# A gated attention and token-MLP block: cutting its last output tile at 384 of 512 columns, and loading W2 in eight DMAs instead of four

## The chip, the cores and the metric

The kernel runs on one core of one Trainium2 chip. The metric is the device time of one execution in microseconds (us).

Engine names in the profile: PE is TensorE (PEld its weight loads), DVE is VectorE, ACT is ScalarE, POOL is GpSimd, SP is SyncE, the engine that issues most of the DMAs here. A `q` after a name (SPq) marks what that engine's sequencer does.

## The reference

```python
# x: [1, 2048, 512] bf16. A: linear attention, 32 heads of 16. B: MLP over tokens, F = 1792.
g = sigmoid((x * gate_w).sum(-1, keepdims=True))
a = attention(x) @ wo                                  # [2048, 512]
u = gelu(einsum("bsd,sf->bdf", layernorm(x), w1) + b1)
b = (einsum("bdf,fs->bds", u, w2) + b2).transpose      # [2048, 512]
return g * a + (1 - g) * b
```

## The kernel before

The output is made in 16 tiles of 128 tokens and 512 columns. For each tile TensorE makes the attention part (`aps`, 4 matmuls) and the MLP part (`yps`, 14 matmuls over F = 14 x 128). ScalarE scales `aps` into `a_sc`, VectorE mixes `yps` and `a_sc` into `ot`, and SyncE stores `ot` by a DMA. The last tile is cut into two parts of 256 columns, so that only half a tile's mix and store follow the last matmul.

```python
NT, D, NF, P, SC, NSC, TPC = 16, 512, 14, 128, 512, 4, 4   # (from the shapes)
...
w2c = []

def load_w2(c):                              # chunk c of W2: 512 tokens, 1.75 MB
    w = wpool.tile([P, NT, FB * P], BF16, name="w2c", tag="wc")
    w2c.append(w)
    nc.sync.dma_start(out=w[:, :NF, :], in_=w2_view[:, :, c * SC : (c + 1) * SC])
...
for t in range(NT):
    c, tl = divmod(t, TPC)
    aps = bank("aps")
    for j in range(ND):
        mm(aps[:], pqT[:, j, t * P : (t + 1) * P], W2sb[:, j, :], j == 0, j == ND - 1)
    a_sc = work.tile([P, D], FP32, name="a_sc", tag="a_sc", bufs=2)
    nc.scalar.activation(out=a_sc[:], in_=aps[:], func=ACT.Identity,
                         scale=gg[:, t : t + 1], bias=c2[:, t : t + 1])
    parts = 2 if t == NT - 1 else 1
    W = D // parts
    for h in range(parts):
        cs = slice(h * W, (h + 1) * W)
        yps = bank("yps")
        for f in range(NF):
            mm(yps[:, :W], w2c[c][:, f, tl * P : (tl + 1) * P], uT[:, f, cs],
               f == 0, f == NF - 1)
        ot = opool.tile([P, D], BF16, name="ot", tag="ot")
        nc.vector.scalar_tensor_tensor(out=ot[:, :W], in0=yps[:, :W],
            scalar=c1[:, t : t + 1], in1=a_sc[:, cs], op0=ALU.mult, op1=ALU.add)
        nc.sync.dma_start(out=o_view[:, t, cs], in_=ot[:, :W])
    ...
```

What the source does not show: the framework gives each DMA that SyncE or ScalarE issues one of eight semaphores, in turn. (A semaphore is a counter that the landing of the DMA raises and that a waiting instruction tests.) At the end of the program SyncE waits for everything by a fixed list of nine waiting instructions. The second to the ninth hold the first to the eighth of these semaphores, always in that order (each also holds one other semaphore, met before). The built program shows that the last store of this kernel has the fourth semaphore, so it stands fifth in the list. Right after the list comes SyncE's first drain, the instruction that the times below call "the drain".

## Time and profile before

The median was 166.06 us in three runs (165.96 to 166.17). The profiled execution had a span of 164.0 us from its first to its last instruction.

These lines are from the page of the profile: the span, TensorE's busy time, the granted clock in 40 slices (tenths), the chain of work that ended last, the group of the mixes (busy us, mean ns of one, idle time before them and what ended it), and the DMA issues of W2 (count, KB each, median us from issue to landing).

```profile
span 164.0 us, 2057 instructions
PE 158.9 (97%) x771; PEld 74.1 (45%) x785; DVE 87.8 (54%) x200; ACT 58.7 (36%) x90; POOL 18.3 (11%) x37
PEclk9999999999999999999999999999999999999999
PE 95%; DMA 2%; issue 1%; ACT 0%; DVE 0%
L472 DVE SCALAR_TENSOR_TENSOR ot<-yps,c,a_sc 128x512 bf16<-128x512 f32 (+1 forms) x17 | 12.2, 719 | 46.1 <-PE yps L108 46.1
w2c<-in_B_w_dram SPq DMA_DIRECT2D x4, 1792.0 KB, 8.8
```

TensorE is busy 97% of the time and is nearly the whole chain. VectorE's 46.1 us of idle time before the mixes are waits for TensorE and cost nothing, except after the last matmul, when there is no more TensorE work to hide behind. So the timeline of the end is the view to read (start us, duration us, engine, line, operation, count, and in brackets the idle time before it):

```profile
157.54 3.22 PE L108 MATMUL yps<-uT,w2c 128*128 128x256 bf16 x28
157.71 3.93 SPq L476 DMA_DIRECT2D out_dram<-ot  x3
159.32 0.48 DVE L472 SCALAR_TENSOR_TENSOR ot<-yps,c,a_sc 128x256 bf16<-128x256 f32 x1 [1.64 <-PE yps L108]
160.80 0.48 DVE L472 SCALAR_TENSOR_TENSOR ot<-yps,c,a_sc 128x256 bf16<-128x256 f32 x1 [0.99 <-PE yps L108]
```

The last mix starts at 160.80 and takes 0.48 us. After it come the last store and the closing waits, over 2.5 us in which no compute engine works. How they stand can be seen when the view of SyncE's instructions at the closing line is asked for the stretch from the store's landing (162.84) to SyncE's drain (163.16). Its columns are the count, the duration in ns (least, median, most), and the first and last start in us:

```profile
L504 SPq EVENT_SEMAPHORE  x5: 28/28/28, 162.9 to 163.1; - x5
```

Five waiting instructions run after the landing. The first is the one that waited for it; the other four wait for nothing any more and still cost about 61 ns each, from one start to the next.

### The profile page before, as it was taken

To read this page: it belongs to the slowest core of one execution; us is meant where nothing else is said; L and a number is where in the kernel's file an instruction comes from. 1 tells how busy PE (TensorE), PEld (TensorE's weight loads), DVE (VectorE), ACT (ScalarE), POOL (GpSimd) and SP (SyncE) were. 2 spreads that over 40 slices of the span, in tenths; PEclk is the share of its full clock that TensorE was granted. 3 is DMA by queue.
4 is the path that set the end of the run, shared out by engine and by line. 5 is a ranking of instruction groups with operands and counts; after the bars stand their busy time and mean duration, and the time that the engine had idled before them with its cause. 6 is when DMAs were issued, how large, how long until landed. Compare 5 with 4: busy or idle time off the path is not lost.

```text
span 164.0 us, 2057 instructions
## 1 busy us (share of the span) xinstructions
PE 158.9 (97%) x771; PEld 74.1 (45%) x785; DVE 87.8 (54%) x200; ACT 58.7 (36%) x90; POOL 18.3 (11%) x37
## 2 busy tenths in 40 slices
PE   7999999999999999999999999999999999999992
PEld 2544444444544444434444444444444444444471
DVE  0599999958999999009994401256211111111131
ACT  3463386658577373212322113111122221111110
POOL 5000710200200000001055500050000000000000
PEclk9999999999999999999999999999999999999999
DMA  4999999999930005800993599932010011101001
GB/s 147 242 213 252 288 297 356 350 348 349 317 86 0 0 0 184 268 0 0 288 293 91 182 306 297 326 129 79 32 36 32 32 36 50 42 32 36 32 32 32
DMA packets 29993, 25.05 MB, mean 153 GB/s; under 512 B 7776, under 2 KB 29408, under 8 KB 29984
## 3 DMA queue, kind: packets, MB, share of 16 engines
q1 hardware_dynamic: 27968, 22.02, 45.0%
q0 software_dynamic: 1440, 2.38, 5.3%
q10 hardware_dynamic: 576, 0.52, 1.1%
q8 instruction: 6, 0.10, 0.3%
q14 instruction: 3, 0.02, 0.0%
HBM read 21.11 MB, written 2.23 MB: 142 GB/s over the span
## 4 chain that ended last, share of the span: by engine, by line
PE 95%; DMA 2%; issue 1%; ACT 0%; DVE 0%
PE uacc L108 29%; PE yps L108 29%; PE qacc L108 8%; PE gacc L108 8%; PE aps L108 8%; PE kacc L108 8%; DMA xs<-in_A_x_dram 2%; PE pt L194 1%; PE denps L108 1%; PE kvps L108 1%; PE wps L108 1%; ACT xT L198 0%; DVE ot L472 0%; PE zps L108 0%; PE pt L323 0%
## 5 line engine op out<-in xcount | busy, mean ns | idle before, releaser
L108 PE MATMUL uacc<-hs,w1c 128*128 128x512 bf16 x218 | 51.6, 379 | 0.4
L108 PE MATMUL yps<-uT,w2c 128*128 128x512 bf16 (+1 forms) x235 | 50.8, 366 | 0.2
L472 DVE SCALAR_TENSOR_TENSOR ot<-yps,c,a_sc 128x512 bf16<-128x512 f32 (+1 forms) x17 | 12.2, 719 | 46.1 <-PE yps L108 46.1
L108 PEld LDWEIGHTS <-w2c 128*128 128x128 bf16 x238 | 23.3, 98 | 25.3
L108 PEld LDWEIGHTS <-w1c 128*128 128x128 bf16 x224 | 21.6, 98 | 26.1 <-issue 0.4
L457 ACT ACTIVATE a_sc<-aps,c,gg 128x512 f32<-128x512 f32 x16 | 12.4, 778 | 46.7 <-PE aps L108 43.0
L317 ACT ACTIVATE uT<-uacc,bcol 128x512 bf16<-128x512 f32 x14 | 9.3, 687 | 27.7 <-PE uacc L108 27.7
L108 PE MATMUL qacc<-xT,wq_sb 128*128 128x512 bf16 x64 | 16.4, 379 | 0.0
L108 PE MATMUL aps<-W2sb,pqT 128*128 128x512 bf16 x62 | 16.2, 379 | 0.1
L108 PE MATMUL kacc<-wk_sb,xT 128*128 128x512 bf16 x63 | 15.9, 379 | 0.1
L108 PE MATMUL gacc<-pk,xs 128*128 128x512 bf16 x62 | 15.5, 379 | 0.1
L244 ACT ACTIVATE hs<-xs,nmr,rstd 128x512 bf16<-128x512 bf16 x16 | 12.8, 804 | 1.9 <-DVE nmr L238 1.9
L204 ACT ACTIVATE e<-qacc 128x512 bf16<-128x512 f32 x16 | 9.6, 597 | 10.1 <-PE qacc L108 10.1
L413 POOL DMA_DIRECT2D rex<-rd_dram x16 | 9.5, 603 | 23.0 <-DVE pqT L415 18.1
L204 ACT ACTIVATE e<-kacc 128x512 bf16<-128x512 f32 x16 | 9.3, 595 | 6.9 <-PE kacc L108 5.6
L208 DVE SCALAR_TENSOR_TENSOR pk<-kacc,e 128x512 bf16<-128x512 f32 x16 | 11.1, 692 | 0.6
L208 DVE SCALAR_TENSOR_TENSOR pqT<-qacc,e 128x512 bf16<-128x512 f32 x16 | 11.1, 692 | 0.6
L228 DVE BATCH_NORM_STATS2 stats<-xs 128x6 f32<-128x512 bf16 x16 | 10.9, 682 | 0.0
L205 DVE TENSOR_SCALAR e<-e 128x512 bf16<-128x512 bf16 x32 | 9.0, 281 | 3.1 <-ACT e L204 3.1
L400 DVE CUSTOM_DVE_ANT_0 junk<-xs,gw_b 128x512 bf16<-128x512 bf16 x16 | 9.8, 683 | 0.0
L108 PEld LDWEIGHTS <-xs 128*128 128x128 bf16 x64 | 6.3, 98 | 7.5
L108 PEld LDWEIGHTS <-pqT 128*128 128x128 bf16 x64 | 6.3, 98 | 7.6
(64 smaller groups left out, 73.2 us busy)
## 6 DMA issues: line engine op xcount, KB each, us to landing
w2c<-in_B_w_dram SPq DMA_DIRECT2D x4, 1792.0 KB, 8.8
w1c<-in_B_w_dram SPq DMA_DIRECT2D x2, 2048.0 KB, 15.5
w1c<-in_B_w_dram SPq DMA_DIRECT2D x3, 1024.0 KB, 12.3
rex<-rd_dram POOLq DMA_DIRECT2D x16, 128.0 KB, 2.9
out_dram<-ot SPq DMA_DIRECT2D x15, 128.0 KB, 1.7
xs<-in_A_x_dram SPq DMA_DIRECT2D x3, 512.0 KB, 5.3
wq_sb<-in_A_wqkv_dram SPq DMA_DIRECT2D x1, 512.0 KB, 6.9
wv_sb<-in_A_wqkv_dram SPq DMA_DIRECT2D x1, 512.0 KB, 10.9
```

The lines of the kernel that those rows point to most:

```text
L108: nc.tensor.matmul(o, lhsT=lhsT, rhs=rhs, start=start, stop=stop, **kw)
L194: nc.tensor.transpose(pt[:, k * P : (k + 1) * P], xs[:, t, k * P : (k + 1) * P], ident[:])
L204: nc.scalar.activation(out=e[:], in_=acc[:], func=ACT.Exp)
L205: nc.vector.tensor_scalar(out=e[:], in0=e[:], scalar1=1.0, scalar2=PHI_EPS, op0=ALU.min, op1=ALU.add)
L208: nc.vector.scalar_tensor_tensor(out=dst, in0=acc[:], scalar=0.0, in1=e[:], op0=ALU.max, op1=ALU.add)
L228: nc.vector.bn_stats(out=stats[:], in_=xs[:, t, :])
L244: nc.scalar.activation(out=hs[:, t, :], in_=xs[:, t, :], func=ACT.Identity, scale=rstd[:, t : t + 1], bias=nmr[:, t : t + 1],)
L317: nc.scalar.activation(out=uT[:, j, :], in_=acc[:], func=ACT.Gelu_apprx_tanh, bias=bcol[:, j : j + 1])
L400: nc.vector.tensor_tensor_reduce(out=junk[:], in0=xs[:, t, :], in1=gw_b[:], scale=1.0, scalar=0.0, op0=ALU.mult, op1=ALU.add, accum_out=gp ...
L413: nc.gpsimd.dma_start(out=rex[:], in_=src.unsqueeze(1).to_broadcast([8, HEAD, SC]))
L457: nc.scalar.activation(out=a_sc[:], in_=aps[:], func=ACT.Identity, scale=gg[:, t : t + 1], bias=c2[:, t : t + 1],)
L472: nc.vector.scalar_tensor_tensor(out=ot[:, :W], in0=yps[:, :W], scalar=c1[:, t : t + 1], in1=a_sc[:, cs], op0=ALU.mult, op1=ALU.add,)
```

## The change

Two edits, both aimed at what follows the last matmul. The last tile is cut into 384 and 128 columns, so that the last mix and the last store are smaller. And each W2 chunk comes in two DMAs: not for the sake of the loads, but because four more DMAs turn the eight semaphores by half a round, which puts the last store on the eighth, whose wait is the last of the list.

```diff
     def load_w2(c):
         w = wpool.tile([P, NT, FB * P], BF16, name="w2c", tag="wc")
         w2c.append(w)
-        nc.sync.dma_start(out=w[:, :NF, :], in_=w2_view[:, :, c * SC : (c + 1) * SC])
+        for f0 in (0, NF // 2):
+            f1 = f0 + NF // 2
+            nc.sync.dma_start(
+                out=w[:, f0:f1, :], in_=w2_view[:, f0:f1, c * SC : (c + 1) * SC]
+            )
...
-        parts = 2 if t == NT - 1 else 1
-        W = D // parts
-        for h in range(parts):
-            cs = slice(h * W, (h + 1) * W)
+        for c0, W in ((0, D - P), (D - P, P)) if t == NT - 1 else ((0, D),):
+            cs = slice(c0, c0 + W)
             yps = bank("yps")
```

## The prediction

> **What bounds the kernel.** TensorE. The page gives PE 97% of a 164.0 us span at full granted clock; the chain that ended last is 95% PE. In the last stage 512-column matmuls start every 216 ns without a hole, so only what follows the last matmul, 3.4 us, can move much. In the trace: the last matmul starts at 160.49; the last VectorE mix (128x256, 0.484 us) at 160.80; its store is issued at 161.31 (0.333 us) and lands by 162.84, 1.53 us after the issue's start. SyncE then ends a list of nine closing waits about 61 ns apart. Four pass before the landing; the fifth holds the last store's semaphore and passes at 162.86; four more follow, to 163.10; the drain is at 163.16, the end at 163.99.
>
> **What the change does.**
>
> 1. *Closing waits.* The new program has four more loads on SyncE. DMA semaphores go round eight in turn, so the last store moves from the fourth to the eighth, which stands last in the closing list. The four waits after the landing become waits before it: eight at 61 ns from about 161.5 end near 162.0, in free time. Saving 163.10 - 162.86 = 0.24 us, on the critical path.
>
> 2. *Smaller last mix.* 0.752 us for 512 columns and 0.484 us for 256 give, by a line, 0.35 us for 128 and 0.62 us for 384 (estimate). Saving 0.13 us. The 384-column mix would end near 160.6, before the last starts at 160.8, and its store's issue near 161.0, before the last store's at 161.2: it blocks nothing.
>
> 3. *PE in the last tile.* Now 28 matmuls of 256 columns at 109 ns. The 128-column matmuls of the key-value product start every 55.5 ns: 14 x (162 + 55.5) against 28 x 109, no change within 0.03 us.
>
> 4. *Smaller last store.* One DMA engine's eight data packets take 188 ns at 512 B and 358 ns at 1 KB; eight of 256 B should take about 105 ns (estimate), 0.08 us less. But the Trainium skill ("DMA: Bandwidth & Descriptors", Specifications) says that below 512 B the engine does a read-modify-write. No 256 B store is in this trace; I let it take back half: 0.04 us saved.
>
> 5. *W2 in two pieces.* Same bytes, same 1 KB rows; four more issues of 0.37 us on an idle SyncE, four more waits on a weight load. Chunks are issued from 61.9 to 98.6 us, land 8 to 11 us later, are first read at 99, 114, 130 and 146 us. Such waits cost PE nothing now. Worth 0.
>
> **Sum.** 0.24 + 0.13 + 0.04 = about 0.41 us: span about 163.6, measured 166.06 to **165.65 us**, eight times in ten between 165.45 and 165.95. Chances: faster by over 2% 0.005, within 2% 0.985, slower 0.01.
>
> **What would show it.** The ninth closing wait is the one that ends with the landing, and the drain follows within 0.1 us (1). The last mix is 128x128, about 0.35 us, from near 160.8 after the 384-column one (2, 3). Landing 1.4 to 1.55 us after the last issue's start (4); over 1.6 us would be small rows or queueing. PE idle at the W2 matmuls stays near 0.2 us (5).
>
> **What would make it wrong.** A read-modify-write of 0.2 us or more; the two last stores, 0.5 us apart instead of 1.5, queueing; SyncE or VectorE still busy with the 384-column part; the run-to-run spread (0.2 us over three runs).

## The result, and the profile after

The changed kernel took 165.69 us in the median (165.30 to 166.15, six runs); before, with the three further runs of the same rounds, took 166.10 us (165.96 to 166.50, six runs). The ratio is 0.9976, with a 95% interval of 0.9956 to 0.9996. By the 2% mark that is "same"; the interval just excludes no gain at all.

From the page of the changed kernel:

```profile
span 163.6 us, 2078 instructions
PE 159.9 (98%) x785; PEld 73.6 (45%) x785; DVE 87.8 (54%) x200; ACT 58.7 (36%) x90; POOL 18.3 (11%) x37
PE 98%; DVE 0%; issue 0%
L474 DVE SCALAR_TENSOR_TENSOR ot<-yps,c,a_sc 128x512 bf16<-128x512 f32 (+2 forms) x17 | 12.2, 720 | 45.9 <-PE yps L108 45.8
w2c<-in_B_w_dram SPq DMA_DIRECT2D x8, 896.0 KB, 7.5
```

The span is 0.4 us shorter. (TensorE's larger busy time is no extra work: the trace of before lacks the records of 14 matmuls, 771 instead of 785.) The end of the timeline, where the 28 matmuls of the last tile carry the form of the first of them:

```profile
157.55 3.22 PE L108 MATMUL yps<-uT,w2c 128*128 128x384 bf16 x28
157.73 3.81 SPq L478 DMA_DIRECT2D out_dram<-ot  x3
160.09 1.08 DVE L474 SCALAR_TENSOR_TENSOR ot<-yps,c,a_sc 128x384 bf16<-128x384 f32 x2 [2.39 <-PE yps L108]
```

TensorE's stretch is as long as before (3.22 us). The two mixes now stand close together, from 160.09 to 161.16. Narrowed to the end, the same view shows the last of them alone:

```profile
160.73 0.81 SPq L478 DMA_DIRECT2D out_dram<-ot  x2
160.81 0.35 DVE L474 SCALAR_TENSOR_TENSOR ot<-yps,c,a_sc 128x128 bf16<-128x128 f32 x1
```

It starts when the last mix started before, and takes 0.35 us instead of 0.48 us. And SyncE at its closing line, from the landing of the last store (162.65) to the drain (162.75):

```profile
L506 SPq EVENT_SEMAPHORE  x1: 27/27/27, 162.7 to 162.7; - x1
L506 SPq DRAIN  x1: 7/7/7, 162.8 to 162.8; - x1
```

One waiting instruction after the landing instead of five. The trace's own records of the closing list say the same in starts, us. The first wait, which holds no semaphore of the eight, passed at 161.687 and 161.587.

| wait for semaphore | before | changed |
|---|---|---|
| 1st | 161.751 | 161.651 |
| 2nd | 161.813 | 161.713 |
| 3rd | 161.877 | 161.777 |
| 4th | **162.858** (last store) | 161.839 |
| 5th | 162.917 | 161.898 |
| 6th | 162.979 | 161.959 |
| 7th | 163.038 | 162.374 (384-column store) |
| 8th | 163.099 | **162.671** (last store) |
| drain | 163.164 | 162.751 |
| end | 163.994 | 163.610 |

To compare kernels without the noise of their beginnings, times are counted below from the first `yps` matmul of the last tile. That point lies 147.70 to 147.71 us after the first `gacc` matmul in all 13 profiled kernels; `gacc` itself starts between 9.60 and 10.17 us, depending on when the first loads land.

| from the trace, us | before | changed |
|---|---|---|
| last tile's first matmul to last matmul | 2.947 | 3.000 |
| last tile's first matmul to last mix | 3.258 | 3.258 |
| last mix | 0.484 | 0.352 |
| issue of the last store to its landing | 1.532 | 1.462 |
| landing to SyncE's drain | 0.323 | 0.097 |
| drain to end | 0.830 | 0.859 |
| **last tile's first matmul to end** | **6.456** | **6.056** |

The gain at the end is 0.400 us: 0.132 of the mix, 0.070 of the store, 0.226 of the waits, less 0.029 that reappears after the drain. These make 0.399; the remaining 1 ns is the step from the mix to the issue.

### The profile page after: what moved, and what is told of

It is laid out like the page before. It is cut to its first block, busy times and chain, and to the rows that moved or that the text cites. A ratio compares the mean times of both kernels' runs of the same rounds, so it can differ in the third digit from the quotient of the medians.

```text
span 163.6 us, 2078 instructions
## 1 busy us (share of the span) xinstructions
PE 159.9 (98%) x785; PEld 73.6 (45%) x785; DVE 87.8 (54%) x200; ACT 58.7 (36%) x90; POOL 18.3 (11%) x37
## 4 chain that ended last, share of the span: by engine, by line
PE 98%; DVE 0%; issue 0%
PE uacc L108 30%; PE yps L108 30%; PE kacc L108 9%; PE aps L108 8%; PE qacc L108 8%; PE gacc L108 8%; PE wps L108 2%; PE pt L194 1%; PE denps L108 1%; PE kvps L108 1%; DVE ot L474 0%; PE zps L108 0%; PE pt L323 0%
## 5 line engine op out<-in xcount | busy, mean ns | idle before, releaser
L108 PE MATMUL yps<-uT,w2c 128*128 128x512 bf16 (+2 forms) x238 | 51.0, 366 | 0.0
L474 DVE SCALAR_TENSOR_TENSOR ot<-yps,c,a_sc 128x512 bf16<-128x512 f32 (+2 forms) x17 | 12.2, 720 | 45.9 <-PE yps L108 45.8
L108 PEld LDWEIGHTS <-w2c 128*128 128x128 bf16 x238 | 22.8, 98 | 25.9
L269 DVE TENSOR_TENSOR zacc<-zacc,pk 128x512 f32<-128x512 f32 x14 | 9.6, 686 | 0.2
L108 PEld LDWEIGHTS <-wq_sb 128*128 128x128 bf16 x64 | 6.3, 98 | 7.5
```

Of the source, the lines that this page charges most:

```text
L108: nc.tensor.matmul(o, lhsT=lhsT, rhs=rhs, start=start, stop=stop, **kw)
L269: nc.vector.tensor_tensor(out=zacc[:], in0=first, in1=pk[:, t, :], op=ALU.add)
```

## The experiments

Main theory: the terms add, and the order of the closing waits is the largest of them. Rival A: the smaller last piece is all, and the waits would be hidden by something else. Rival B: the finer W2 loads feed TensorE sooner. The first four runs shared a chip and eleven runs of before; the next three and the last four likewise.

### The changed kernel again

No edit.

> The changed kernel once more, to have it timed beside the parts on one chip. All theories: ratio to before near 0.9976 (0.996 to 0.999). In the trace, from the start of the last mix to SyncE's drain: 1.94 us as in its first profile (2.37 us before), of which landing to drain 0.10 us (0.32 us before), mix 0.35 us (0.48 us before), issue to landing 1.46 us (1.53 us before), each within 0.05 us.

Measured: 165.81 us (165.25 to 166.12, six runs) against 166.28 us, ratio 0.9972 (0.9950 to 0.9993). Last mix to drain 1.943 us, landing to drain 0.097, mix 0.351, issue to landing 1.467. So the end repeats within 5 ns, although this execution's span was 0.3 us longer. Where that came from is a line of its timeline of TensorE near the start:

```profile
6.24 0.81 PE L108 MATMUL kacc<-wk_sb,xT 128*128 128x512 bf16 x3 [0.37 <-DMA wk_sb<-in_A_wqkv_dram]
```

TensorE waited 0.37 us for a first load of the attention weights, and the first `gacc` started at 10.13 instead of 9.85 us. Variations of this kind are as large as the whole effect, and no part of the change touches them.

### W2 in two pieces alone

```diff
 # last tile as before: 256 and 256 columns
-        nc.sync.dma_start(out=w[:, :NF, :], ...)
+        for f0 in (0, NF // 2): nc.sync.dma_start(out=w[:, f0 : f0 + NF // 2, :], ...)
```

> W2 in two pieces each, last tile still in 256 and 256 columns. Main theory (order of the closing waits): landing to drain falls from 0.32 to 0.08-0.10 us; mix stays 0.48 us and issue to landing 1.53 us; last mix to drain 2.13-2.15 us, so some 0.23 us less than before, ratio near 0.9986. Rival A (all the gain is the smaller last piece): landing to drain may change, but last mix to drain stays within 0.05 us of 2.37, ratio 1.000. Rival B (finer W2 loads feed TensorE sooner): the last matmul starts over 0.1 us earlier than in before.

Measured: 165.87 us (165.48 to 166.14), ratio 0.9978 (0.9957 to 0.9999). SyncE at its closing line from the landing (162.842) to the drain:

```profile
L508 SPq EVENT_SEMAPHORE  x1: 28/28/28, 162.9 to 162.9; - x1
L508 SPq DRAIN  x1: 13/13/13, 162.9 to 162.9; - x1
```

Landing to drain is 0.097 us; mix (0.485) and landing (1.533) are as before; last mix to drain is 2.143 us, 0.225 less than before, as the main theory said. Rival A falls. Rival B falls too: the last matmul starts at 160.484 us, in before at 160.485, with the first `gacc` at 9.833 in both. Time comes back after the drain here as well (0.866 us, 0.036 more than in before), so to the end the gain is 0.188 us (6.268 against 6.456).

### The 384 and 128 columns alone

```diff
 # W2 in one piece as before
-        parts = 2 if t == NT - 1 else 1
+        for c0, W in ((0, D - P), (D - P, P)) if t == NT - 1 else ((0, D),):
```

> 384 and 128 columns, W2 in one piece each; the last store has the fourth semaphore again. Main theory: mix 0.35 us, issue to landing 1.46 us, but landing to drain 0.32 us as before: last mix to drain about 2.17 us, so 0.20 us less than before, ratio near 0.9988. Rival A: the whole 0.4 us, ratio near 0.9976. There is one catch: the 384-column store now has the third semaphore and lands 0.3 us before the last one, so it should not matter.

Measured: 165.98 us (165.49 to 166.19), ratio 0.9981 (0.9961 to 1.0001). From the landing (162.730) to the drain:

```profile
L502 SPq EVENT_SEMAPHORE  x5: 28/28/28, 162.7 to 163.0; - x5
L502 SPq DRAIN  x1: 7/7/7, 163.1 to 163.1; - x1
```

Mix 0.351, issue to landing 1.483, landing to drain 0.323 us: last mix to drain 2.184, expected about 2.17. To the end it gains 0.184 us (6.272). The two halves of the change make 0.188 + 0.184 = 0.372 us of its 0.400 us. Most of the rest is the scatter of one landing: the same last store took 1.483 us here and 1.462 us in the changed kernel. The timed runs cannot tell either half from the whole.

### The same turn of the semaphores without touching W2

```diff
 # W2 whole, last tile 256 and 256 columns
-            nc.sync.dma_start(out=o_view[:, t, cs], in_=ot[:, :W])
+            if 8 <= t < 12:
+                nc.sync.dma_start(out=o_view[:, t, 0:P], in_=ot[:, 0:P])
+                nc.sync.dma_start(out=o_view[:, t, P:D], in_=ot[:, P:D])
+            else:
+                nc.sync.dma_start(out=o_view[:, t, cs], in_=ot[:, :W])
```

> W2 whole and 256 and 256 columns as before; instead tiles 8 to 11 are each stored by two DMAs (128 columns, then 384), which also makes four more DMAs and moves the last store to the eighth semaphore. Main theory: the same as e1 in the tail: landing to drain 0.08-0.10 us, last mix to drain 2.13-2.15 us, ratio near 0.9986. Rival B: nothing gained, 1.000. It also gives four stores of 256-byte rows with no store of the same time ahead: if these rows cost a read-modify-write, they land no sooner after their issue than 512-byte rows (1.53 us); if they go by size, about 1.45 us.

Measured: 165.69 us (165.38 to 166.46), ratio 0.9975 (0.9950 to 0.9999). Landing to drain 0.081 us, last mix to drain 2.126 us (expected 2.13 to 2.15), to the end 6.221 us: 0.235 us less than before, with W2 as it was. So it is the count of DMAs that matters, not what they carry. This time no 0.03 us came back after the drain (0.835).

The four stores of 256-byte rows in the middle of the stage landed 1.44 to 1.47 us after the start of their issue, the last 512-byte rows of this run 1.53 us, the 1 KB rows before and after them in this stage 1.69 to 1.71 us (apart from the first three stores of the stage, which took longer). The store's DMA line and the landing line of the view of the output tile, narrowed to the first of them:

```profile
L477 SPq DMA_DIRECT2D out_dram<-ot x1: 333/333/333, 134.7 to 134.7; - x1
DMA to landing us min/median/max: 1.5/1.5/1.5
```

The trace has 1.474 us for this one. Time goes by size down to 256 bytes a row; no read-modify-write penalty shows.

### One more load: the last store on the first semaphore

```diff
 # the changed kernel, W2 chunk 0 in three pieces
-        for f0 in (0, NF // 2):
+        for f0, f1 in ((0, 5), (5, 10), (10, NF)) if c == 0 else ((0, 7), (7, NF)):
```

> The changed kernel, but the first W2 chunk comes in three pieces: one more load, and the last store moves on from the eighth semaphore to the first, which stands second of the nine closing waits. Main theory: seven waits are left after the landing, so landing to drain is 7 x 0.061 + 0.08 = about 0.5 us (0.10 us in the changed kernel), last mix to drain about 2.35 us (1.94 us): the change's whole gain is given back, ratio to before near 1.000. Mix 0.35 us and issue to landing 1.46-1.48 us unchanged. Rival A (order of waits is worth nothing): last mix to drain stays at 1.94 us and the ratio near 0.9975. Rival B (finer W2 loads): the same or a little better than the changed kernel.

Measured: 166.81 us (166.40 to 167.06) against 166.23 us, ratio 1.0031 (1.0016 to 1.0046). This is slower than expected; the ratio near 1.000 was missed. From the landing (162.565) to just after the drain:

```profile
L505 SPq EVENT_SEMAPHORE  x8: 27/28/28, 162.6 to 163.0; - x8
L505 SPq DRAIN  x2: 13/72/130, 163.1 to 163.6; - x2
```

Eight waits stand after the landing (the one that it released, and seven more); landing to drain is 0.559 us, last mix to drain 2.392 us. That much was expected (0.5 and 2.35 us), and rivals A and B are refuted once more. But then SyncE stands: its first drain is at 163.12 and its second only at 163.59. In the other kernels there are 0.05 to 0.08 us between these two. Drain to end became 1.350 us instead of 0.859.

I then looked at SyncE's instructions in the traces of all kernels, counted from the first recorded one. Each kernel with 82 or 83 of them (changed, again, `e1`, `e4`, `e5`, `e6`) has a gap of 0.45 to 0.48 us before its 80th. In the changed kernel the 80th is the wait for a release that the other engines pass 0.33 us earlier (162.956 against 163.289), and all but about 0.03 us of the pause is hidden. In `e4`, one instruction longer, the 80th is the drain by which SyncE reports to the others, and nothing hides it. The kernels with 75 to 79 (before, `e2`, `e3`) do not reach that place. (Their last instruction also has 0.45 to 0.46 us before it, but that is a wait for GpSimd's last release, which ScalarE, VectorE and TensorE pass within 12 ns of SyncE.) This was a new theory: the pause belongs to a place in SyncE's program. `e7`, `e8` and `e9` below test it.

### A still smaller last piece: 448 and 64 columns

```diff
-        for c0, W in ((0, D - P), (D - P, P)) if t == NT - 1 else ((0, D),):
+        for c0, W in ((0, D - 64), (D - 64, 64)) if t == NT - 1 else ((0, D),):
```

> The changed kernel with 448 and 64 columns: where does a smaller last piece stop paying? By the line through the measured mixes the 448-column mix takes 0.69 us and the 64-column one 0.28 us; the rows of the last store are 128 B. If the mix were all (naive reading): 0.07 us less from last matmul to drain. I expect a loss: TensorE has at most 14 x 55 = 0.78 us of work after the 448 columns (less if 64-column matmuls go faster), the 448-column mix is not done before the last one could start, and SyncE still issues its store (0.33 us) then. The last mix starts 0.2 to 0.35 us later than in the changed kernel, counted from the first matmul of the last tile, the last store is issued over 0.2 us later in spite of the shorter mix. Issue to landing 1.40-1.46 us. The spacing of the 64-column matmuls (27 ns if by columns, 55 ns if the weights set a floor) is measured by the way.

Measured: 165.75 us, a single run. The end of its timeline:

```profile
157.43 3.22 PE L108 MATMUL yps<-uT,w2c 128*128 128x448 bf16 x28
160.33 0.88 DVE L474 SCALAR_TENSOR_TENSOR ot<-yps,c,a_sc 128x448 bf16<-128x448 f32 x2 [2.76 <-PE yps L108]
```

The last mix takes only 0.275 us, but it starts 3.506 us after the last tile's first matmul instead of 3.258, behind the 448-column mix (0.684 us). The last store is issued at 4.041 us instead of 3.638, behind the issue of the 448-column store. Issue to landing was 1.474 us, a little over the expected range. To the end it takes 6.477 us: the whole gain of the change is gone. The 64-column matmuls started every 29 to 30 ns, so new weights set no floor of 55 ns.

### Three parts: 256, 160 and 96 columns

```diff
-        for c0, W in ((0, D - P), (D - P, P)) if t == NT - 1 else ((0, D),):
+        for c0, W in ((0, 256), (256, 160), (416, 96)) if t == NT - 1 else ((0, D),):
 # and W2 chunk 3 in one piece, so that there are four extra DMAs again
```

> A try at beating both: the last tile in 256, 160 and 96 columns, three W2 chunks in two pieces, so that the last store stays on the eighth semaphore. If 96-column matmuls start every 41 ns, TensorE's work is unchanged; the 160-column mix (0.38 us) is done before the last starts; the last mix takes 0.32 us (0.35 us), the 192-byte rows land 0.01-0.02 us sooner: last tile's first matmul to drain 0.04 to 0.06 us shorter than in the changed kernel, far too little for the timed runs to tell (ratio near 0.997). If weights set a floor of 55 ns, the 96-column part takes 0.2 us longer on TensorE and the version loses 0.15 us against the changed kernel.

Measured: 165.75 us (165.37 to 166.06) against 166.23 us, ratio 0.9968 (0.9952 to 0.9984). From its timeline:

```profile
160.21 0.38 DVE L473 SCALAR_TENSOR_TENSOR ot<-yps,c,a_sc 128x160 bf16<-128x160 f32 x1 [0.43 <-PE yps L108]
160.80 0.32 DVE L473 SCALAR_TENSOR_TENSOR ot<-yps,c,a_sc 128x96 bf16<-128x96 f32 x1 [0.21 <-PE yps L108]
```

VectorE is idle for 0.21 us before the last mix, so the part ahead does not block it; the 96-column matmuls start every 42 to 43 ns. Last tile's first matmul to drain is 5.158 us, 0.039 us less than in the changed kernel (5.197), just under the 0.04 to 0.06 us expected; to the end 6.018 us.

### The extra DMAs as stores, with 384 and 128 columns

```diff
 # the changed kernel, with W2 whole again
-        for f0 in (0, NF // 2): ...
+        nc.sync.dma_start(out=w[:, :NF, :], in_=w2_view[:, :, c * SC : (c + 1) * SC])
 # and the stores of e3
+            if 8 <= t < 12:
+                nc.sync.dma_start(out=o_view[:, t, 0:P], in_=ot[:, 0:P])
+                nc.sync.dma_start(out=o_view[:, t, P:D], in_=ot[:, P:D])
```

> The changed kernel with its four extra DMAs made otherwise: W2 whole, tiles 8 to 11 stored by two DMAs each; 384 and 128 columns, last store on the eighth semaphore. SyncE's program is three instructions shorter than in the changed kernel. Theory of the place in the program (SyncE stands for 0.45-0.48 us before its 80th recorded instruction, in every kernel that has 82 or more of them): with 79 the pause is not there, drain to end 0.83 us (0.86 us), landing to drain 0.08 us, last tile's first matmul to end 6.00-6.02 us (6.06 us in the changed kernel). Rival (the pause belongs to the finer W2 loads or to the semaphore's place): 6.06 us again. Ratio near 0.997.

Measured: 165.85 us (165.61 to 166.13) against 166.17 us, ratio 0.9984 (0.9969 to 0.9999). SyncE has 79 recorded instructions and no pause; drain to end 0.836 us, landing to drain 0.081 us. Last tile's first matmul to end is 6.026 us, 6 ns outside the expected range and 0.030 us less than in the changed kernel. Of this gain 0.023 us lie after the drain; 0.016 us lie before it (0.081 against 0.097, for a reason that no run shows), and 0.009 us are lost again in the landing.

### Five extra loads, the fifth issued by ScalarE

```diff
 # e4, but:
+            q = nc.scalar if (c, f0) == (0, 10) else nc.sync
-            nc.sync.dma_start(
+            q.dma_start(
                 out=w[:, f0:f1, :], in_=w2_view[:, f0:f1, c * SC : (c + 1) * SC]
```

> The kernel with five extra loads (last store on the first semaphore), but the fifth of them issued by ScalarE, so that SyncE's program is as long as in the changed kernel. Separates two costs that came together there: seven waits left after the landing, and 0.45 us that SyncE stood between its two drains. Theory of the place in the program: landing to drain 0.50-0.56 us as there, but drain to end 0.86 us in place of 1.35 us; ratio to before near 1.000 in place of 1.003. Rival (the 0.45 us comes with the semaphore's place): drain to end 1.35 us, ratio 1.003.

Measured: 166.04 us (165.89 to 166.23, five runs) against 166.17 us, ratio 0.9996 (0.9981 to 1.0010). From the landing (162.405) to just after the second drain:

```profile
L506 SPq EVENT_SEMAPHORE  x8: 28/28/28, 162.4 to 162.9; - x8
L506 SPq DRAIN  x2: 7/7/7, 163.0 to 163.0; - x2
```

Eight waits and 0.559 us to the drain as in `e4`, but both drains within 0.06 us, and drain to end 0.866 us. The pause moved back behind the second drain, before SyncE's 80th instruction. The two costs that came together in `e4` are separated: the place of the semaphore gives back the whole gain of the change and 0.068 us more (6.524 us to the end, 6.456 in before), and the one instruction more in SyncE's program costs another 0.476 us (7.000).

### Twelve extra loads

```diff
-        for f0 in (0, NF // 2):
+        for f0, f1 in ((0, 4), (4, 8), (8, 11), (11, NF)):
```

> The changed kernel with each W2 chunk in four pieces: twelve extra loads instead of four, so the last store is on the eighth semaphore again, and SyncE's program is eight instructions longer than the changed kernel's. Theory of the place: the pause of 0.45 us is still before the 80th recorded instruction, which is now the fourth closing wait, before the landing: hidden; drain to end 0.83 us, last tile's first matmul to end 6.02-6.04 us. Rival (the pause is tied to the end of the program): 6.06 us, pause after the second drain. Main theory of the closing waits: landing to drain 0.08-0.10 us whether four or twelve loads are extra.

Measured: 165.72 us (165.43 to 165.82, five runs), ratio 0.9972 (0.9958 to 0.9987). SyncE has 90 recorded instructions. The gap of 0.44 us stands before the 80th, now the fourth closing wait (162.006 to 162.450), before the landing at 162.909, where it costs nothing. Landing to drain 0.082, drain to end 0.830 us; to the end 6.013 us, a little better than expected. The pause is tied to the place, not to the end of the program, and a full extra turn of the semaphores changes nothing.

### The best of both

```diff
 # e7, but:
-            if 8 <= t < 12:
+            if 8 <= t < 11:
-        for c0, W in ((0, D - P), (D - P, P)) if t == NT - 1 else ((0, D),):
+        for c0, W in ((0, 256), (256, 160), (416, 96)) if t == NT - 1 else ((0, D),):
```

> The best of both: last tile in 256, 160 and 96 columns, W2 whole, tiles 8 to 10 stored by two DMAs each (three extra DMAs and one of the last tile). Last tile's first matmul to end 5.96-5.98 us: 6.018 us of the three parts with W2 loads, less 0.03 us of the pause and 0.016 us of landing to drain. Before has 6.456 us, the changed kernel 6.056 us. Ratio near 0.9965; against the changed kernel the timed runs cannot tell 0.08 us.

Measured: 165.66 us (164.98 to 165.92) against 166.17 us, ratio 0.9965 (0.9946 to 0.9985). The landing of its last two stores, from the view of the output tile narrowed to them:

```profile
L478 SPq DMA_DIRECT2D out_dram<-ot x2: 332/332/332, 161.0 to 161.5; - x2
DMA to landing us min/median/max: 1.4/1.5/1.5
```

Last tile's first matmul to end is 5.979 us, within the range expected, 0.477 us less than before and 0.077 us less than the changed kernel. In the traces it is the shortest of all. The timed runs do not tell it from the changed kernel, so that it beats the changed kernel is shown for the end of the trace only. (With 80 recorded SyncE instructions its 80th is the last wait of all, where a pause and the wait for GpSimd cannot be told apart.)

The ends of all thirteen traces together, in us:

| kernel | waits after landing | mix | issue to landing | landing to drain | drain to end | last tile's first matmul to end |
|---|---|---|---|---|---|---|
| before | 5 | 0.484 | 1.532 | 0.323 | 0.830 | 6.456 |
| changed | 1 | 0.352 | 1.462 | 0.097 | 0.859 | 6.056 |
| `e0` changed again | 1 | 0.351 | 1.467 | 0.097 | 0.859 | 6.061 |
| `e1` W2 only | 1 | 0.485 | 1.533 | 0.097 | 0.866 | 6.268 |
| `e2` split only | 5 | 0.351 | 1.483 | 0.323 | 0.829 | 6.272 |
| `e3` more stores | 1 | 0.484 | 1.534 | 0.081 | 0.835 | 6.221 |
| `e4` first semaphore | 8 | 0.351 | 1.455 | 0.559 | 1.350 | 7.000 |
| `e5` 448 and 64 | 1 | 0.275 | 1.474 | 0.096 | 0.866 | 6.477 |
| `e6` three parts | 1 | 0.318 | 1.423 | 0.096 | 0.860 | 6.018 |
| `e7` stores, 384 and 128 | 1 | 0.351 | 1.471 | 0.081 | 0.836 | 6.026 |
| `e8` fifth on ScalarE | 8 | 0.351 | 1.462 | 0.559 | 0.866 | 6.524 |
| `e9` twelve loads | 1 | 0.350 | 1.462 | 0.082 | 0.830 | 6.013 |
| `e10` stores, three parts | 1 | 0.316 | 1.421 | 0.082 | 0.839 | 5.979 |

## Why the prediction was right or wrong

The predicted time was 165.65 us with a range of 165.45 to 165.95; measured were 165.69 us and, in the later rounds, 165.81 us. The mechanism was right, and the terms were nearly the right size.

1. **Closing waits: right.** 0.24 us was predicted; landing to drain fell by 0.226 us. The built program shows the order of the semaphores, and the trace of before shows the price of a wait, so this could be computed. `e1` and `e3` show the term alone, `e4` and `e8` reverse it. Two things were missed beside it. The list does not end near 162.0 us: the eighth wait stops for the 384-column store until 162.374, still 0.28 us before the landing. And 0.029 us come back after the drain, because the longer SyncE program runs into the pause that `e7` to `e9` place.
2. **Smaller last mix: right.** 0.13 us predicted by a line through two measured sizes, 0.132 measured (0.484 to 0.352). The 384-column mix and its store's issue block nothing, as said: the last mix starts 3.258 us after the tile's first matmul in both kernels. `e5` shows where that ends.
3. **TensorE in the last tile: right.** The spacing is 162 to 163 and 55 to 56 ns, as estimated. The last matmul starts 0.053 us later, but as a shorter one it is done at the same time.
4. **Smaller last store: right in sign, too small.** 0.04 us predicted, 0.070 measured (0.049 to 0.077 over the seven traces with this last store). The half that I gave to the read-modify-write, which the Trainium skill states ("DMA: Bandwidth & Descriptors", Specifications), did not appear: 1.462 us for 256-byte rows against 1.532 for 512-byte rows, and 1.44 to 1.47 with no store just ahead (`e3`). The DMA records agree: from the first data packet to the first semaphore packet, which is the time of one DMA engine's eight data packets, it took 110 ns at 256 B, near the 105 ns estimated without a penalty, against 188 ns at 512 B. The first packet only came about 0.02 us later after the issue (0.85 to 0.86 us against 0.83). The other store, 0.46 us ahead, costs at most about 0.04 us by these numbers.
5. **W2 in two pieces: right.** Worth nothing as loads: the stretch from the first `gacc` to the last tile is 147.70 to 147.71 us with 4, 7, 8, 9 or 16 loads of W2. The 0.2 us of idle TensorE before the W2 matmuls that the prediction expected to stay shows only in the four traces that lack records of such matmuls (before, `e4`, `e5`, `e6`); in the changed kernel and the others it is 0.0.

The sum of the predicted terms was 0.41 us; the trace has 0.400 us. That the two are so close is in part luck: the store gained 0.03 us more than predicted, and the 0.03 us after the drain, not foreseen, took as much away. Luck, too, is a median within 0.04 us of the one predicted, as the same kernel gave 165.81 us in the later rounds. (The prediction's "3.4 us" after the last matmul is a slip: it is 3.51 us from that matmul's start and 3.24 us from its end.) The chance of a visible change (over 2%) was rightly put near zero. What the prediction said least well is the scatter: single runs of the changed kernel went from 165.25 to 166.15 us, wider than the range given for the median. The beginnings of the profiled executions differ by up to 0.57 us (first `gacc` at 9.60 to 10.17 us), which would make most of such a scatter.

Open: what the pause of 0.44 to 0.48 us before SyncE's 80th recorded instruction is. The runs show its place, not its cause. No DMA record of an instruction load falls into it, but one follows it: in each of the nine kernels with 80 or more recorded SyncE instructions, the first instruction load after 160 us (a packet of 8 KB) starts 0.62 to 0.88 us after the start of the 80th, in `e9` (163.27 us) as in the changed kernel (163.91 us). In the four shorter ones it starts 1.1 to 1.9 us after the last recorded instruction. So a load of instructions goes with this place in the program; whether the load is SyncE's, and whether the pause has to do with it, is not shown.

## What to carry to other kernels

When one engine is busy to the end, read what follows its last instruction line by line: the last mix, the store's issue and landing, the closing waits. Each of them is paid in full, and a piece can be made smaller only until the piece ahead of it gets in its way. Count the DMAs: which semaphore the last store gets decides how many empty waits follow its landing, and any extra DMA that SyncE or ScalarE issues turns it, wherever it stands; here the spread from the landing to the drain was from 0.08 to 0.56 us. And for an effect of a few tenths of a us, compare intervals inside the traces from a common event, not spans or times.

## What the Trainium skill lacked or had wrong

- "DMA: Bandwidth & Descriptors", Specifications, says that below 512 B the engine does a read-modify-write. For stores of 128 rows from SBUF to HBM no penalty shows down to 192 bytes a row: about 1.70 us from issue to landing at 1 KB, about 1.53 at 512 B, 1.44 to 1.48 at 256 B, 1.42 at 192 B. (At 128 B, in one run, 1.474 us.) One DMA engine's eight packets go by size as well: 188 ns at 512 B, 110 at 256 B, 91 at 192 B, 73 at 128 B. What short rows do to bandwidth is not tested here.
- The same page, in its anatomy of one DMA (for the path that GpSimd issues), puts most of about 2 us of fixed cost down to the write receipt. For a store issued by SyncE the last one of before has 0.83 us from the start of the issue (0.50 us from its end) to the first data packet, 0.34 us of packets, and 0.36 us from the last packet's end to the last semaphore increment. For this path the page gives a first-byte latency (about 0.6 us, Specifications), but no split of the rest.
- No page that I read has the price of the closing waits or their order: about 61 ns for each wait already satisfied, and 0.08 to 0.56 us from the last landing to the drain, by the semaphore that the last store happens to get.
- "Runtime: NRT & Kernel Launch", Instruction fetch mechanics, says that instructions are refilled in blocks and that crossing a boundary is mostly hidden. SyncE stands 0.44 to 0.48 us before its 80th recorded instruction in every kernel here that has 82 or more of them, hidden or not depending on where that falls (`e8` 0.866 us and `e4` 1.350 us from drain to end). Whether this is such a boundary no run here shows; that an 8 KB instruction load starts 0.62 to 0.88 us after the 80th instruction fits it.
